# The order of every operation of an attention-and-mixer kernel written out as a list, in place of a list scheduler's choice

## The chip, the cores and the metric

The kernel runs on one core of a Trainium2 chip. The metric is device time in microseconds (us) of one execution, lower is better. A core has five engines that run at the same time: PE (TensorE, matrix products), ACT (ScalarE), DVE (VectorE), POOL (GpSimd) and SP (SyncE). Each takes its own instructions in the order in which the program issued them; semaphores tie the engines to each other. POOL and SP here issue almost only DMAs, ACT a few.

## The reference

Two networks, one behind the other, on q, k, v of 8 batches × 8 heads × 576 rows × 64:

```python
scores = scale * np.matmul(q, k.transpose(0, 1, 3, 2))
bias = slopes[:, None, None] * (-np.abs(rel).astype(np.float32))[None, :, :]
mask = (rel >= 0) & (rel < window)            # window = 128
scores = np.where(mask, scores + bias[None], -1000000000.0)
attn = softmax(scores);  out = np.matmul(attn, v)
x = out.transpose(0, 2, 1, 3).reshape(B, S, H * D)          # 8 x 576 x 512
xt = x.transpose(0, 2, 1)
h = np.maximum(xt @ w_tok1, 0.0) @ w_tok2                    # 576 -> 256 -> 576
u = x + h.transpose(0, 2, 1)
h2 = np.maximum(u @ w_ch1, 0.0) @ w_ch2                      # 512 -> 1536 -> 512
return u + h2
```

So a causal attention with a window of 128 and a bias that falls with the distance, then a mixer over the 576 tokens, then one over the 512 channels. Inputs and output are float32.

## The kernel before, in words

Products are in bf16 with float32 sums in PSUM. The 576 rows of a batch are four blocks of 128 and a tail of 64. Batches are worked on in pairs, and the two tails of a pair share one block (`TAIL`). `opening` does the attention and token mix of batch 0 by pairs of heads, so that work can start on the first loads. Then, for each batch `b`, `main(b)` is the channel mixer of that batch and `side(b + 1)` the attention and token mix of the next; their operations are interleaved. A block of `side` goes: loads by POOL; q and k turned, by a DMA transpose that SP issues (L761) or by products with the identity on PE (L772); scores (L809); exponential on ACT (L824) and mask on DVE (L834); value product (L897), whose 65th column is the sum; reciprocal (L910) and normalization, on DVE (L913, one operation) or ACT (L919, one for each head). The token mix has the products with W1 (L944) and W2, and `u` is written to `ub` (L1005) and turned by SP (L1013). `main` multiplies `uT` with WC1 in units (L1402, L1502), copies and adds what comes out on ACT or DVE (L1417, L1418, L1426 to L1430, L1508, L1509), and multiplies with WC2 (L1679).

In the opening the pairs of heads have their own lines: bias by a product (L1089), turns (L1063), scores (L1106), values (L1149), the score, value and normalization of the tail (L1194, L1220, L1227), and the token mix (L1243 with W1 and L1248 with its last 64 rows `W1p`, L1271 with W2). POOL's loads there are `load_pair` (L623, L630), `weights` (L635) and `load` (L614).

Nothing is issued directly. Each step is recorded as an operation (`plan.op`), 1486 in all, with its engine, a cost in ns, what it needs, the buffers it makes and uses, a rank, and sometimes a second engine that could do it (`other`). Buffers come from rings of a few slots: `ps` (8 PSUM banks), `qk`, `v`, `qkT`, `pe`, `rt`, `r`, `s`, `raw` and more; in the lists below `v_72` is a slot. A buffer's next owner has to wait for the last reader of the one before it.

`Plan.run` is a list scheduler. It steps through a modelled time; for each engine it takes the ready operation that can start earliest, ties going to the lower rank; it chooses the engine of operations with two, and the slot that is free first. POOL's operations keep one fixed order (`slot()`). A table, `NUDGES`, shifts the rank of single operations or holds them until a modelled time ("611:-21079:100923" is operation 611, rank, time); random shifts of the ranks are there too, with seeds that are all 0. `Plan.emit` then issues everything in order of the modelled start, and puts matmuls of a tile of zeros (`spin`, L1737) into those idle stretches of the modelled PE that begin before a set time, 60 us, and are longer than 250 ns, where a bank is free:

```python
        for a, z in self.gaps:
            if a < FILL and z - a > 250:
```

```python
    plan.run()
    plan.emit(spin)
```

Of the kernel before, what the change touches and what calls it, by code (L numbers as in the profile page):

```python
# [16 lines left out]
SEM = 40.0  # L17
# [54 lines left out]
class Plan:  # L72
# [60 lines left out]
    def run(self):  # L133
        ops = self.ops
        for item in NUDGES.split():
            n, rank, after = item.split(":")
            ops[int(n)].rank += float(rank)
            ops[int(n)].after = max(ops[int(n)].after, float(after))
        dice = [random.Random(x) for x in SEEDS]
        for o in ops:  # L140
            if SEEDS[o.part]:
                o.rank += dice[o.part].uniform(-SHIFT, SHIFT)
        succ = {o: [] for o in ops}
        left, held = {}, []
        ready = {o: o.after for o in ops}
        cand = {e: [] for e in ("PE", "ACT", "DVE", "POOL", "SP")}

        def enter(o):
            if any(x.t0 is None for x in o.behind):
                held.append(o)  # L150
                return
            cand[o.eng].append(o)
            if o.other:
                cand[o.other[0]].append(o)

        for o in ops:
            left[o] = len(o.deps)
            for d in o.deps:
                succ[d].append(o)
            if not o.deps:  # L160
                enter(o)
        pool = sorted((o for o in ops if o.eng == "POOL"), key=lambda o: o.order)
        free = dict(FREE)
        lanes, sent, turns = [], 0, []
# [5 lines left out]
        def finish(o):  # L170
            for h in list(held):
                if o in h.behind and all(x.t0 is not None for x in h.behind):
                    held.remove(h)
                    enter(h)

        def release(o):
            for s in succ[o]:
                left[s] -= 1
                ready[s] = max(ready[s], free["PE"] if o.eng == "PE" == s.eng else o.done + SEM)
                if not left[s]:  # L180
                    enter(s)

        def advance(to):
            nonlocal clock, flying
            while True:
# [11 lines left out]
                both = lines[0] and lines[1]  # L197
                rate = BOTH[lines[1][0][1].bus > 0] if both else (1.0, 1.0)
# [17 lines left out]
        def send(o, at, line, work, late):  # L216
            nonlocal flying
            coming.append([at, line, work, o, late])
            flying += 1

        while todo:
            best = None
            for e, c in cand.items():
                pick, early = None, None
                for o in c:
                    if e == "POOL" and o is not pool[sent]:
                        continue
                    t = max(ready[o], free[e])
                    if e == "DVE" and (o.narrow or last[0]):
                        t = max(t, last[1] + 31.0)  # L230
                    if o.other:
                        mine, its = (o.cost, o.other[1]) if e == o.eng else (o.other[1], o.cost)
                        that = o.other[0] if e == o.eng else o.eng
                        if max(ready[o], free[that]) + its < t + mine - (0 if e == o.eng else 1):
                            continue
                    asked = []
                    for b in o.bufs:
                        if b.slot is None:
                            opts = b.options()
                            got = b.ring.best(opts, asked.count(opts))  # L240
                            asked.append(opts)
                            if got is None:
                                t = None
                                break
                            t = max(t, got[0])
                    if t is None:
                        continue
                    if e == "POOL" and len(lanes) >= 8:
                        if lanes[-8].done is None:
                            continue  # L250
                        t = max(t, lanes[-8].done)
                    if e == "SP" and o.bus > 0 and len(turns) > 1 and turns[-2].done is None:
                        continue
                    own = o.rank - (ALIKE if e == "PE" and o.mode == mode != 0 else 0)
                    key = (t if t > free[e] + 1e-6 else free[e], own, o.n)
                    if pick is None or key < pick[0]:
                        pick = (key, o)
                    if o.rank < FIRST and (early is None or key < early[0]):
                        early = (key, o)
                if early and early[1] is not pick[1] and early[0][0] < pick[0][0] + GRACE * pick[1].cost:  # L260
                    pick = early
                if pick and (best is None or pick[0][0] < best[0][0]):
                    best = pick + (e,)
# [155 lines left out]
ALIKE = 0  # L419
# [1352 lines left out]
```

## Time and profile before

| what | value |
|---|---|
| times of the runs, us | 273.66, 274.33, 275.8; median 274.33 |
| span of the profiled execution, us | 272.2 (no time of this execution beside its span is given) |
| last matmul ends, us from the span's start | 268.53 |
| PE busy, matmuls recorded / weight loads | 263.6 us (97%), 2965 / 2992 |
| DVE, ACT, POOL busy | 224.7 (83%), 150.7 (55%), 114.7 (42%) |
| share of the chain that ended last | PE 90%, DMA 3%, POOL 3% |
| granted TensorE clock | 1.00 in every stretch looked at |

The span runs from the first to the last instruction of the core; the time is counted from outside and is longer. Every matmul comes with a weight load of its own, so the count of weight loads is that of matmuls; 27 matmuls have no record. A row of the lists of waits says which engine and line stood idle, what released it, and then us in total, times and the longest. In a timeline, a row's "x4" puts several instructions of a kind together.

### The profile page before, as it was taken

The numbers are of one execution on the slowest core, as the hardware profiler recorded it, in microseconds if no ns is written. First come the engines' busy times: TensorE is split into PE (matmuls) and PEld (weight loads), VectorE is DVE, ScalarE is ACT, GpSimd is POOL, SyncE is SP. The second block draws the span as 40 slices with busy tenths as digits, with TensorE's granted clock in tenths as the row PEclk, the third lists the DMA queues.
The fourth block names the chain that finished last, engine by engine and source line by source line (L and its number), as shares of the span: only waits on it lengthen the run. The fifth ranks groups of instructions, "written<-read, shape, count | busy, mean of one in ns | idle before, by whom it ended". The sixth has DMA issues, their size and how long they took to land.

```text
span 272.2 us, 7391 instructions
## 1 busy us (share of the span) xinstructions
PE 263.6 (97%) x2965; PEld 191.8 (70%) x2992; DVE 224.7 (83%) x520; ACT 150.7 (55%) x267; POOL 114.7 (42%) x147
## 2 busy tenths in 40 slices
PE   7989999999999999999999999999999999999994
PEld 5767566676686655587786756498886758589883
DVE  7887699978897569688999478698998989976983
ACT  6973796226881298107992089308973089506700
POOL 8978796840397007800870307800651050004000
PEclk9999999999999999999999999999999999999999
DMA  8999999999999979999999999999999580035005
GB/s 201 178 173 180 167 148 183 157 156 175 186 127 161 192 162 78 137 119 210 200 149 119 142 228 96 140 154 142 212 132 67 110 239 2 2 82 171 4 10 183
DMA packets 160338, 38.59 MB, mean 142 GB/s; under 512 B 146544, under 2 KB 159472, under 8 KB 160304
## 3 DMA queue, kind: packets, MB, share of 16 engines
q0 software_dynamic: 109968, 19.64, 89.4%
q1 hardware_dynamic: 49104, 17.70, 33.4%
q10 hardware_dynamic: 1232, 0.79, 1.0%
q8 instruction: 23, 0.38, 0.5%
q14 instruction: 11, 0.09, 0.1%
HBM read 35.85 MB, written 9.44 MB: 166 GB/s over the span
## 4 chain that ended last, share of the span: by engine, by line
PE 90%; DMA 3%; POOL 3%; issue 1%; ACT 1%; DVE 0%; POOLq 0%
PE ps L1679 27%; PE ps L1502 15%; PE ps L1402 12%; PE ps L897 6%; PE ps L809 5%; PE ps L987 4%; PE ps L944 4%; PE ps L1545 4%; PE ps L1590 4%; DMA W<-in_moe_w_tok_dram 2%; POOL v L623 1%; DMA qkT<-qk 1%; POOL qk L630 1%; PE ps L772 1%; PE ps L1488 1%
## 5 line engine op out<-in xcount | busy, mean ns | idle before, releaser
L614 POOL DMA_DIRECT2D v<-in_v_dram x36 | 30.5, 849 | 76.4 <-PE ps L897 72.8
L824 ACT ACTIVATE pe<-ps 128x1024 bf16<-128x1024 f32 (+1 forms) x56 | 51.3, 969 | 3.1 <-PE ps L809 3.0
L1502 PE MATMUL ps<-uT,WC 128*128 128x512 bf16 x182 | 46.0, 379 | 0.7 <-issue 0.2
L1508 ACT ACTIVATE r<-ps 128x512 bf16<-128x512 f32 x45 | 26.4, 601 | 35.9 <-PE ps L1502 33.8
L1679 PEld LDWEIGHTS <-r 128*128 128x128 bf16 x384 | 36.8, 98 | 7.4 <-issue 0.7
L1679 PEld LDWEIGHTS <-s 128*128 128x128 bf16 x288 | 27.8, 98 | 5.8 <-DVE s L1527 0.4
L614 POOL DMA_DIRECT2D qk<-in_k_dram x35 | 30.3, 873 | 3.7 <-DMA qk<-in_k_dram 1.6
L834 DVE TENSOR_TENSOR pe<-pe,mask 128x1024 bf16<-128x1024 bf16 (+1 forms) x48 | 30.5, 650 | 1.6 <-ACT pe L824 1.4
L614 POOL DMA_DIRECT2D qk<-in_q_dram x35 | 30.2, 867 | 3.7 <-DMA qkT<-qk 1.7
L1502 PEld LDWEIGHTS <-WC 128*128 128x128 bf16 x196 | 17.7, 98 | 18.1 <-issue 0.5
L1417 ACT COPY raw<-ps 128x512 f32<-128x512 f32 x27 | 15.5, 597 | 22.6 <-PE ps L1402 22.6
L1679 PE MATMUL ps<-WC,r 128*128 128x256 bf16 x192 | 24.9, 273 | 0.0
L1679 PE MATMUL ps<-WT,s 128*128 128x256 bf16 x192 | 24.7, 273 | 0.0
L1679 PE MATMUL ps<-WT,r 128*128 128x256 bf16 x192 | 23.8, 273 | 0.1
L897 PEld LDWEIGHTS <-pe 128*128 128x128 bf16 (+1 forms) x480 | 19.5, 99 | 5.6 <-DVE pe L834 0.8
L1426 DVE TENSOR_TENSOR r<-ps,raw 128x512 bf16<-128x512 f32 x30 | 20.2, 680 | 3.3 <-ACT raw L1417 2.8
L897 PE MATMUL ps<-v,pe 128*128 128x65 bf16 (+1 forms) x480 | 22.8, 194 | 0.1
L1005 DVE TENSOR_TENSOR ub<-ps,xb 128x512 bf16<-128x512 f32 x32 | 20.5, 683 | 2.7 <-ACT r L1508 0.9
L913 DVE TENSOR_TENSOR xb<-ps,rt 128x256 bf16<-128x256 f32 (+1 forms) x52 | 21.4, 417 | 0.5
L1650 DVE TENSOR_TENSOR raw<-ps,ub 128x512 f32<-128x512 f32 x25 | 17.0, 686 | 5.8 <-PE ps L1679 5.8
L1402 PE MATMUL ps<-tt,WS 128*128 128x256 bf16 x132 | 18.8, 273 | 0.1
L809 PEld LDWEIGHTS <-qkT 64*128 64x128 bf16 x448 | 11.9, 94 | 8.3 <-issue 5.9
(143 smaller groups left out, 479.4 us busy)
## 6 DMA issues: line engine op xcount, KB each, us to landing
out_dram<-raw SPq DMA_DIRECT2D x19, 256.0 KB, 4.4
qk<-in_q_dram POOLq DMA_DIRECT2D x30, 128.0 KB, 5.4
qk<-in_k_dram POOLq DMA_DIRECT2D x30, 128.0 KB, 5.4
v<-in_v_dram POOLq DMA_DIRECT2D x28, 128.0 KB, 5.1
WC<-in_moe_w_ch_dram POOLq DMA_DIRECT2D x8, 384.0 KB, 7.5
out_dram<-raw POOLq DMA_DIRECT2D x6, 256.0 KB, 3.4
out_dram<-ob SPq DMA_DIRECT2D x5, 256.0 KB, 4.1
v<-in_v_dram POOLq DMA_DIRECT2D x16, 64.0 KB, 4.8
```

The costliest lines, as they stand in the source:

```text
L614: nc.gpsimd.dma_start(out=to()[p0 : p0 + n, :, :], in_=rows(src, b, s0, n))
L809: pe_.matmul(wide(e)[:, i, kind, a:z], lhsT=ts[kb]()[e * D : (e + 1) * D, NHP + i, :], rhs=ts[blk]()[e * D : (e + 1) * D, i, a:z], start=T ...
L824: act_.activation(out=pb()[:, e, :, lo:, c0:c1_], in_=wide(e)[:, :, lo:, c0:c1_], func=ACT.Exp, scale=scale)
L834: dve_.tensor_tensor(out=o, in0=o, in1=heads(mk, es), op=ALU.mult)
L897: pe_.matmul(view()[a:z, at, i, :], lhsT=pb()[:, e, i, kind, a:z], rhs=vb()[:, h, 0 : D + 1], start=m == 0, stop=m == len(mms) - 1, skip_g ...
L913: dve_.tensor_tensor(out=x4(), in0=view()[r0:r1_, :, :, 0:D], in1=rt()[r0:r1_, 0:n, :, :].broadcast_to([r1_ - r0, n, 4, D]), op=ALU.mult)
L1005: plan.op("DVE", 690, lambda blk=blk, ht=ht, hs=hs: dve_.tensor_tensor(out=ub()[:, blk, :], in0=ht()[:, hs], in1=xb()[:, blk, :], op=ALU.a ...
L1402: pe_.matmul(bk()[:, c * HS : (c + 1) * HS], lhsT=l(c, cb), rhs=r(cb), start=new and c == 0 and cb == 0, stop=cb == 1, skip_group_check=True)
L1426: add = plan.op("DVE", 690, lambda: dve_.tensor_tensor(out=o(), in0=half_of(bk), in1=half_of(e), op=ALU.add), rk + UNIT_RANK, uses=[bk, e] ...
L1502: pe_.matmul(ct()[:, :], lhsT=WC1[:, cb, t * P : (t + 1) * P], rhs=uT()[:, cb, :], start=cb == 0, stop=cb == NCB - 1)
L1508: plan.op("ACT", 600, lambda t=t, ct=ct: act_.activation(out=r2()[:, t, :], in_=ct()[:, :], func=ACT.Relu), rk, part=(r2, t), uses=[ct], o ...
L1679: pe_.matmul(bk()[:, c * HN : (c + 1) * HN], lhsT=l(t, c), rhs=w(t), start=first, stop=g == 1 and t == HK - 1, skip_group_check=True)
```

## The change

The scheduler goes. `Plan.follow` takes three tables: `ORDER`, the numbers of all 1486 operations (in base 36) in the order in which they are placed; `ELSEWHERE`, the operations that run on their second engine; and `PLACES`, the first slot of each buffer in the order in which buffers first appear. Each engine's queue is what `ORDER` leaves for it. A replay of that order, with the same costs as before and two more waits in the model (280 ns after POOL's lane, 650 ns after a transpose on SP), gives each operation a modelled start, and `emit` still issues by these and still fills modelled gaps of PE. `NUDGES`, `SEEDS`, `SHIFT`, `FIRST`, `GRACE` and `ALIKE` are gone. No operation is added or removed; 59 run on the other engine, and the fills go from 52 matmuls to 49. The file is 20 lines shorter ahead of the code, so a line L1220 of before is L1200 now.

```diff
-    def run(self):
-        ops = self.ops
-        for item in NUDGES.split():
...
+    def follow(self):
+        def number(x):
+            return int(x, 36)
+
+        ops, seq = self.ops, [self.ops[number(x)] for x in ORDER.split()]
+        assert sorted(o.n for o in seq) == list(range(len(ops)))
+        for x in ELSEWHERE.split():
+            o = ops[number(x)]
+            o.eng, o.cost, o.emit = o.other
+        line = {e: [o for o in seq if o.eng == e] for e in ("PE", "ACT", "DVE", "POOL", "SP")}
...
+        places = iter(PLACES)
+        for o in seq:
+            for b in o.bufs:
+                if b.slot is None:
+                    first = number(next(places))
+                    b.slot = tuple(range(first, first + len(b.choice[0])))
+                    for i in b.slot:
+                        if b.ring.owner[i]:
+                            behind[o].append(b.ring.owner[i])
+                        b.ring.owner[i] = b
+                        b.ring.log[i].append(b)
+        ready, free = {o: o.after if o.after < 9e3 else 0.0 for o in ops}, dict(FREE)
...
+        def earliest(e, o):
+            if left[o] or any(u.done is None for b in behind[o] for u in b.users):
+                return None
+            t = max([ready[o], free[e]] + [u.done + SEM for b in behind[o] for u in b.users])
...
         while todo:
             best = None
...
+            for e, q in line.items():
+                if at[e] < len(q):
+                    t = earliest(e, q[at[e]])
+                    if t is not None and (best is None or t < best[0]):
+                        best = (t, e)
...
-NUDGES = ("611:-21079:100923 615:-377:0 618:6245:106227 624:11583:0 628:-3532:0 631:-20512:118175 632:4405:0 "
...
+ORDER = ("m i 52 4z d g 7 8 f 9 e a 4v 4x h k j n o l 1 2 6 4w 4y 3 50 51 5 57 53 55 58 56 c b 5c 59 5a 54 5b 5d 5i 5f "
...
+ELSEWHERE = ("4w 4y 5m 63 6f 6i 6x 7b 7m 84 86 88 8o 8q a5 at b6 bc bd c0 c2 c4 c8 ce cg cm cy fc fp fs fw gh gj gl gn gp "
...
-    plan.run()
+    plan.follow()
     plan.emit(spin)
```

The tables move instructions on every engine. Three places follow, each as it stands in before and then as it stands now.

POOL, the loads of the opening: `W_120` is W1, `W_122` W2, `W1p` the last 64 rows of W1, and the `v` buffers hold the values of batch 0's pairs of heads and its tail. Before:

```order
L623 DMA v_74<-in_v_dram 128x4x64 x2
L630 DMA qk_70<-in_q_dram 128x2x256
L630 DMA qk_70<-in_k_dram 128x2x256
L614 DMA v_73<-in_v_dram 64x8x64
L635 DMA W_120<-in_moe_w_tok_dram 128x4x256
L635 DMA W1p<-in_moe_w_tok_dram 64x256
L623 DMA v_75<-in_v_dram 128x4x64 x2
L623 DMA v_76<-in_v_dram 128x4x64 x2
L635 DMA W_122<-in_moe_w_tok_dram 128x2x512
```

Now:

```order
L610 DMA qk_68<-in_q_dram 128x2x256
L610 DMA qk_68<-in_k_dram 128x2x256
L603 DMA v_73<-in_v_dram 128x4x64
L615 DMA W_120<-in_moe_w_tok_dram 128x4x256
L603 DMA v_72<-in_v_dram 128x4x64 x2
L615 DMA W_122<-in_moe_w_tok_dram 128x2x512
L603 DMA v_75<-in_v_dram 128x4x64
L594 DMA v_76<-in_v_dram 64x8x64
L603 DMA v_75<-in_v_dram 128x4x64
L615 DMA W1p<-in_moe_w_tok_dram 64x256
```

W2 has moved ahead of the last three loads of values, the tail's values (64x8x64) have moved back from ahead of W1 to next to last of them, and W1's last rows have moved behind them all.

PE, at the end of the tail's value products (`pe_84` and `pe_86` hold the tail's exponentials, `pe_85` a block's). Before:

```order
L1220 MATMUL ps<-v_76,pe_84 64x65
L1220 LDWEIGHTS pe_84
L1220 MATMUL ps<-v_73,pe_84 64x65
L1737 LDWEIGHTS zero
L1737 MATMUL ps<-zero 128x512
L1737 LDWEIGHTS zero
L1737 MATMUL ps<-zero 128x512
L1737 LDWEIGHTS zero
L1737 MATMUL ps<-zero 128x128
```

Now:

```order
L1200 MATMUL ps<-v_75,pe_86 64x65
L1200 LDWEIGHTS pe_86
L1200 MATMUL ps<-v_76,pe_86 64x65
L1223 LDWEIGHTS W_120
L1223 MATMUL ps<-xb_91,W_120 128x128
L1223 LDWEIGHTS W_120
L1223 MATMUL ps<-xb_91,W_120 128x128
```

Two blocks of eight products with W1 stood ahead of the tail's value products; now all of them stand behind, the first of them where two wide and five narrow products with `zero` stood, and three narrow ones follow it. Further on, near 43 us of the span before, six narrow products with `zero` stood between the last value product of a tail (L897) and the token mix (L944); there are none after the opening now, and the token mix's first products stand among the value products of other blocks.

SP, around the transposes of one batch's `u` in the middle of the program (`uT`, `uTt`). Before:

```order
L1606 DMA out_dram<-raw_105 64x512 x2
L1013 DMA_TRANSPOSE uTt_100<-ub_93 128x4x128
L1013 DMA_TRANSPOSE uT_99<-ub_93 128x4x128 x4
L761 DMA_TRANSPOSE qkT_78<-qk_69 128x8x128
L761 DMA_TRANSPOSE qkT_83<-qk_71 128x8x128
L1662 DMA out_dram<-raw_107 128x2x256
L761 DMA_TRANSPOSE qkT_77<-qk_67 128x8x128
```

Now:

```order
L741 DMA_TRANSPOSE qkT_77<-qk_70 128x8x128
L741 DMA_TRANSPOSE qkT_78<-qk_71 128x8x128
L1642 DMA out_dram<-raw_105 128x2x256
L1642 DMA out_dram<-ob_109 128x2x256
L1642 DMA out_dram<-raw_106 128x2x256
L741 DMA_TRANSPOSE qkT_80<-qk_67 128x8x128
L1642 DMA out_dram<-raw_104 128x2x256
L1586 DMA out_dram<-raw_108 64x512
L1642 DMA out_dram<-raw_107 128x2x256
L741 DMA_TRANSPOSE qkT_79<-qk_69 128x8x128
L993 DMA_TRANSPOSE uT_98<-ub_93 128x4x128 x4
L993 DMA_TRANSPOSE uTt_100<-ub_93 128x4x128
```

The transpose that came first behind the `uT` group (`qkT_78` before) is the one just ahead of it now (`qkT_79`), and two more that followed the group now precede it (`qkT_80`, `qkT_77`).

More of the change, by code (lines that the diff above doesn't have):

```diff
@@ L131, in dma @@
         return o
-    def run(self):
-        ops = self.ops
-        for item in NUDGES.split():
[L136 to L139, printed above, removed]
-        for o in ops:
[L141 to L157, printed above, removed]
+    def follow(self):
[7 more added lines that the diff above has]
+        line = {e: [o for o in seq if o.eng == e] for e in ("PE", "ACT", "DVE", "POOL", "SP")}
+        succ = {o: [] for o in ops}
+        left = {o: len(o.deps) for o in ops}
+        behind = {o: [] for o in ops}
+        for o in ops:
@@ L168, in run @@
         lines, coming, clock, flying = ([], []), [], START, 0
[L170 to L174, printed above, removed]
         def release(o):
@@ L221, in run @@
         while todo:
             best = None
[L223 to L263, printed above, removed]
@@ L267, in run @@
             assert best, ("stuck", todo)
[L268 to L273 removed]
+            t, e = best
+            o = line[e][at[e]]
+            at[e] += 1
             todo -= 1
[L275 to L277 removed]
             if e == "PE":
```

98 lines of the change are left out of this document (34 added, 64 removed), and 42 rows, old and new, of the table ORDER.

## The prediction, made before the changed kernel was run

> **What bounds the kernel now.** The page first: busy shares over the whole span.
>
> ```profile
> span 272.2 us, 7391 instructions
> PE 263.6 (97%) x2965; PEld 191.8 (70%) x2992; DVE 224.7 (83%) x520; ACT 150.7 (55%) x267; POOL 114.7 (42%) x147
> ```
>
> TensorE (PE) is busy for 97% of the span. Its weight loads number 2992 and its matmuls 2965, so 27 matmul records are missing, and some of the 8.6 us (272.2 − 263.6) that look idle are not. The table by stage says where idle time can be at all (each row: stretch, its length, then busy time and count of PE, weight load, DVE, ACT, POOL, the granted clock, DMA share, GB/s).
>
> ```profile
> 0.00:20.00 20.00, 17.30 (x295) 12.95 (x295) 16.38 (x60) 15.15 (x29) 17.55 (x28) 1.00 1.44 184
> 30.00:100.00 70.00, 69.42 (x761) 46.08 (x771) 57.78 (x131) 40.98 (x71) 35.60 (x44) 1.00 1.75 169
> 100.00:150.00 50.00, 49.13 (x554) 35.99 (x558) 44.35 (x102) 29.09 (x50) 22.53 (x27) 1.00 1.38 138
> 150.00:240.00 90.00, 89.37 (x957) 64.09 (x966) 76.57 (x171) 51.11 (x93) 27.50 (x35) 1.00 1.02 128
> 240.00:268.53 28.53, 28.53 (x285) 25.58 (x283) 21.65 (x42) 10.12 (x18) 2.86 (x4) 1.00 0.27 84
> 268.53:272.20 3.67, 0.00 (x0) 0.00 (x0) 0.42 (x1) 0.00 (x0) 0.00 (x0) 1.00 0.40 119
> ```
>
> The first 20 us hold 2.70 us of idle PE. The three long stretches show 0.58, 0.87 and 0.63, together 2.08 us in 210, at the full granted clock. The last 28.5 us hold none, and the 3.67 us behind the last matmul are an add and a store that the change leaves in their order. PE's own waits name the causes (releaser; us in total, times, longest).
>
> ```profile
> PE ps L1737 <- DVE zero L565: 1.0, 1, 1.0
> PE ps L1243 <- DMA W<-in_moe_w_tok_dram: 0.6, 1, 0.6
> PE ps L1220 <- ACT pe L1114: 0.5, 1, 0.5
> PE ps L809 <- DMA qkT<-qk: 0.4, 1, 0.4
> ```
>
> The first is the start of the program and stays. The others are the largest idle times that a better order could remove (smaller ones follow in that view); beside them stand the matmuls on `zero`, which are time that PE spends on nothing.
>
> **The change part by part.** The same 532 groups of PE work are issued in both kernels. Matmuls go from 2992 to 2989, all of it fills (52 to 49), so the real work is 2940 in each. The change can move the time only through idle time, through fills and through the engines that PE waits for.
>
> *The opening.* The chain of waits (start, us, what):
>
> ```profile
> 8.19 5.95 DMA W<-in_moe_w_tok_dram
> ...
> 17.37 0.67 PE ps L1220 x16
> 18.03 0.82 PE ps L1737 x7
> 18.85 0.56 PE ps L1149 x14
> 19.40 0.34 PE ps L1737 x6
> 19.74 0.33 PE ps L1248 x4
> ```
>
> W1's load is issued at 8.19 and releases PE at 14.13; that 0.6 wait goes, since W1's first product now stands behind L1220. What ends last there instead are the v loads that L1220 reads. POOL issued them, and W2, so (start, us; then size and us to landing, from the issues near 12.5 us):
>
> ```profile
> 9.60 3.02 POOL L623 DMA_DIRECT2D v<-in_v_dram  x4
> 12.56 0.75 POOL L635 DMA_DIRECT2D W<-in_moe_w_tok_dram  x1
> W<-in_moe_w_tok_dram POOLq DMA_DIRECT2D x1, 256.0 KB, 5.6
> v<-in_v_dram POOLq DMA_DIRECT2D x1, 64.0 KB, 4.2
> ```
>
> The last v load is issued at about 9.60 + 3.02 × 3/4 = 11.9 and lands at 11.9 + 4.2 = 16.1; W2, next in line, lands at 12.56 + 5.6 = 18.2. So 256 KB cost the line 18.2 − 16.1 = 2.1 us. In the new order W2 stands ahead of the last three loads that L1220 reads and W1's 32 KB tail goes behind them. The last of them lands near 16.1 + 2.1 − 0.2 = 18.0 (32 KB at that rate are 0.26), where PE had L1220 done at 17.37 + 0.67 = 18.04. Since only L1220's last products read it, L1220 ends about 0.1 later. Behind L1220 the fills (0.82 + 0.34 = 1.16) are partly replaced by two blocks of W1 products that stood ahead of it, but the product that follows, L1248 at 19.74, waits for DVE's norm of L1220's result, 1.7 us after its end, in either order. The cover for the moved blocks is therefore this gap, and what they free lies ahead of L1220, where the v load now decides. I take −0.2 for the opening. The ends: −1.1 if the v loads come in time (0.6 of wait and 0.5 of wait both gone), +0.7 if the last v load comes a whole 64 KB (2.1 / 4 = 0.5) behind W2, at 18.2 + 0.5 = 18.7.
>
> Four wide bias matmuls also move out of the first five microseconds. Their prices (start, us; then the same line later):
>
> ```profile
> 2.59 2.32 PE L1089 MATMUL ps<-dist,slant 128*128 128x128 bf16 x12 [0.24 <-DVE slant L582]
> 8.19 0.60 PE L1089 MATMUL ps<-dist,slant 128*128 128x256 bf16 x4
> ```
>
> The early twelve are 8 of 256 columns and 4 of 128, 2560 columns or 0.91 ns each; the later four take 0.60 / 1024 = 0.59 ns a column. Early there are now 6 wide and 2 narrow, 768 columns fewer, worth 768 × 0.32 = 0.25 us, but fills take their place there and the qk loads set when the next work starts, so I count 0, between −0.25 and 0. [...]
>
> *The fill at 43 us.*
>
> ```profile
> 43.05 0.69 PE L897 MATMUL ps<-v,pe 128*64 128x65 bf16 x16
> 43.68 0.51 PE L1737 MATMUL ps<-zero 128*128 128x128 bf16 x6
> 44.04 1.24 PE L944 MATMUL ps<-xb,W 128*128 128x512 bf16 x4
> ```
>
> From 43.68 to 44.04 PE multiplies zeros while DVE normalizes the tail that L944 waits for. Now L944's first products are spread among the value products and no fill stands there: −0.4, or 0 if the wait remains and merely shows as idle.
>
> *The transposes near 121 us.*
>
> ```profile
> 115.07 6.03 SPq L1013 DMA_TRANSPOSE uT<-ub  x4
> 121.27 2.61 SPq L761 DMA_TRANSPOSE qkT<-qk  x2
> 124.52 0.23 PE L809 MATMUL ps<-qkT 64*128 64x128 bf16 x2 [0.42 <-DMA qkT<-qk]
> ```
>
> SP issues in its own order, so qkT waited behind the 6.03 us of uT, and L809 stood 0.42 for it. In the new order this qkT and two more go out ahead of the uT group: −0.4. What is late next is uT itself, pushed by one issue, 2.61 / 2 = 1.3 us, if SP reaches the new place only when `ub` is ready; its first reader would then wait up to 1.3. SP's rows show it waiting for `ub`, not being late for it, so the issue fits into that wait:
>
> ```profile
> SPq L1013 <- DVE ub L1005: 56.2, 8, 18.7
> ```
>
> *Operations on their other engine (59).* Prices, mean ns of one:
>
> ```profile
> L1418 DVE COPY raw<-ps 128x512 f32<-128x512 f32 x3 | 2.1, 686 | 0.0
> L913 DVE TENSOR_TENSOR xb<-ps,rt 128x256 bf16<-128x256 f32 x50 | 20.6, 417 | 0.5
> L1417 ACT COPY raw<-ps 128x512 f32<-128x512 f32 x27 | 15.5, 597 | 22.6 <-PE ps L1402 22.6
> L919 ACT ACTIVATE xb<-ps,rt 128x64 bf16<-128x64 f32 x48 | 11.1, 333 | 0.5 <-DVE rt L910 0.4
> ```
>
> DVE takes 14 more full-bank copies and relus at about 0.686 = 9.6, and loses 12 half-bank operations at 0.417 (8 norms and 4 copies of uT) = 5.0 and two relus at 0.686 = 1.4: about +3.2 us. ACT takes 32 pieces of norms at 0.333 = 10.7 and seven copies and relus at about 0.6 = 4.2, and loses 16 at 0.6 = 9.6: about +5.3. ACT's 55% hide that; a moved norm takes 4 × 0.333 = 1.3 on ACT where DVE took 0.417, which is covered only while PE has other work. DVE is the tighter:
>
> ```profile
> 116.00:146.00 30.00, 29.33 (x371) 23.96 (x372) 27.39 (x63) 19.82 (x36) 11.04 (x13) 1.00 1.46 167
> ```
>
> Here 2.6 us of 30 are free on DVE. The 3.2 us are spread over some 200 us, so they fit on average; for new short waits I add +0.2, between 0 and +1.6 (half of the 3.2).
>
> The sum: −0.2 − 0.4 − 0.4 + 0.2 = −0.8 us. No time of the profiled execution but its span is given; the median of the runs, 274.33, lies 2.1 above it, and the same is taken to lie around the new one. So 274.33 − 0.8 = 273.5, a span of about 271.4.
>
> **The rivals.**
>
> *A larger gain.* The v loads come in time and every small idle goes: −1.1 in the opening, −0.25, −0.4, −0.4, and half of the 2.08 us less the 0.42 already counted, −0.8; together −2.9, 271.4, and 270.5 to 272.5 around it. For it: no wait of PE after 20 us but L809's is over 0.4. Against it: the missing 27 records at about 0.11 us are 3.0 us, more than all idle after 20 us, so there may be little to gain. A row shows how dense the work is (chain; 48 matmuls of 256 columns):
>
> ```profile
> 239.65 5.24 PE ps L1679 x48
> ```
>
> That is 109 ns each, back to back. [...]
>
> *DVE becomes the bound.* If half of its added work falls where DVE has no room, +1.6 more on the path than none: 273.5 + 1.4 = 274.9, and 274.5 to 276.0. It decides from 2.6 us more in such a 30 us stretch. For it: 91% there. Against it: norms leave DVE in the same stages.
>
> *Slower: POOL's queue holds.* POOL issues loads in order, and a v load waits until PE has read the old v:
>
> ```profile
> POOL v L614 <- PE ps L897: 72.8, 12, 15.7
> qk<-in_k_dram POOLq DMA_DIRECT2D x30, 128.0 KB, 5.4
> ```
>
> A k load behind it needs 5.4 us to land and some 3 us as a transpose before PE can use it, about 8.5. The new order mixes loads of several blocks. If one such k load is released 8.5 − 4 = 4.5 us or less before its use instead of in time, PE stands some 4 us: 273.5 + 4 = 277.5 (276 to 278). It decides once a release comes later than 8.5 us before the product. Against it: with the old queue the only such wait was 0.42, and qkT mostly goes out earlier now.
>
> *No effect.* Every gain is taken back by the next thing in line, since loads and norms and not the list set the moments: 274.3.
>
> **How the numbers follow.** About 1% (2.7 us) is what a measurement tells from no change here; the three runs alone differ by 2.1. The forecast has 0.45 (272.5 to 274.5), the larger gain 0.22, DVE 0.18, POOL 0.09, no effect 0.06. Faster by over 1% is below 271.6: some 0.6 of the larger gain, 0.13. Slower by over 1% is above 277.1: most of POOL's and a little of DVE's, 0.10. Within 1%: 0.77. The range leaves out the lower half of the larger gain (0.1) and POOL's (0.09): 271.4 to 276.0.
>
> **What would show it.** Right: no L809 wait for qkT near 121 us; no `zero` matmul after 21 us; L1200 (the new number of L1220) ending within 0.3 us of 18.0 and waiting for a v load; PE busy 97% again. Wrong: in the opening, L1200 ending after 18.7 or before 17; in the middle, PE waits named DVE of over 0.5 us together (DVE's rival); a new wait for qkT of over 1 us (POOL's). If the last matmul ends before 265.6 or after 271.3, the sum has missed a term.

## The result, and the profile after

| | before | after |
|---|---|---|
| median of the runs, us | 274.37 (6 runs, 273.66 to 275.8) | 278.47 (6 runs, 277.13 to 280.29) |
| ratio, 95% interval | | 1.0155 (1.0123 to 1.0188) |
| span of the profiled execution, us | 272.2 | 275.9 (the time of that run is 277.71, 1.8 above) |
| mean granted clock, all runs | 1.000 in the profiled one | 0.985 to 0.994 |

The kernel became slower by 4.1 us; 273.5 had been forecast. The first lines of the page of the kernel after:

```profile
span 275.9 us, 7370 instructions
PE 264.5 (96%) x2962; PEld 192.5 (70%) x2989; DVE 228.1 (83%) x521; ACT 151.8 (55%) x290; POOL 114.6 (42%) x147
```

PE's busy time rose by 0.9 us and the span by 3.7, so most of the loss is idle PE. DVE has 3.4 us more, ACT 1.1. The stretches (columns as in the prediction) show where the idle time is:

```profile
0.00:20.00 20.00, 17.31 (x277) 12.75 (x278) 14.91 (x51) 14.60 (x28) 16.11 (x26) 0.91 1.44 183
8.00:12.00 4.00, 4.00 (x57) 2.80 (x54) 2.40 (x4) 2.22 (x4) 3.81 (x6) 0.59 1.58 188
20.00:30.00 10.00, 9.85 (x139) 7.60 (x140) 7.48 (x21) 5.42 (x14) 10.00 (x13) 1.00 1.96 165
30.00:100.00 70.00, 66.49 (x730) 44.57 (x740) 56.28 (x124) 42.05 (x77) 39.26 (x50) 1.00 1.61 147
100.00:150.00 50.00, 49.53 (x559) 35.58 (x564) 44.94 (x104) 29.18 (x55) 20.50 (x25) 1.00 1.53 165
150.00:240.00 90.00, 89.27 (x959) 64.64 (x967) 76.08 (x169) 53.06 (x104) 25.87 (x33) 1.00 1.01 130
```

From 30 to 100 us PE stands 3.51 us where it stood 0.58; from 100 on the stretches are as dense as before. And there is a second, smaller sign at the beginning: PE is just as busy in the first 20 us, but at a mean clock of 0.91; from 8 to 12 us it was granted 0.59. PE's waits name the large idle time:

```profile
PE ps L1482 <- DMA WC<-in_moe_w_ch_dram: 2.1, 1, 2.1
PE ps L1043 <- DVE qk L627: 1.1, 2, 0.9
PE ps L789 <- DVE qkT L758: 0.6, 1, 0.6
```

The first is a wait for a load of the channel mixer's weights, WC1; no such wait was in the profile before. It stands at 30.20 to 32.29 us, and the third right behind it (timeline of PE, start and duration, in brackets the idle time ahead):

```profile
29.82 0.38 PE L1468 MATMUL ps<-uT,WC 128*128 128x512 bf16 x1
32.29 1.04 PE L1482 MATMUL ps<-uT,WC 128*128 128x512 bf16 x4 [2.09 <-DMA WC<-in_moe_w_ch_dram]
33.88 0.23 PE L789 MATMUL ps<-qkT 64*128 64x128 bf16 x2 [0.55 <-DVE qkT L758]
```

L1482 is the line that was L1502: one chunk of `main(0)`, four products with 128 columns of WC1. Before, it began at once, at 29.28:

```profile
29.28 1.02 PE L1502 MATMUL ps<-uT,WC 128*128 128x512 bf16 x4
```

POOL's timeline shows why the load is late (L615 issues weights, L594 a load of q, k or v):

```profile
13.67 0.81 POOL L615 DMA_DIRECT2D WC<-in_moe_w_ch_dram  x1
16.17 0.82 POOL L615 DMA_DIRECT2D WC<-in_moe_w_ch_dram  x1
19.30 0.89 POOL L594 DMA_DIRECT2D v<-in_v_dram  x1 [2.30 <-PE ps L1200]
...
25.41 0.80 POOL L615 DMA_DIRECT2D WC<-in_moe_w_ch_dram  x1
```

WC1 comes in four loads of 384 columns (384 KB each). The third of them is issued at 25.41, behind seven loads of v, q and k, of which the first stood 2.30 us for PE to read the old v. From the issues near 25.4:

```profile
WC<-in_moe_w_ch_dram POOLq DMA_DIRECT2D x1, 384.0 KB, 6.8
```

25.41 + 6.8 = 32.2, where L1482 starts. In the kernel before the first three of these loads went out at 13.24, 16.44 and 18.98:

```profile
13.24 0.83 POOL L635 DMA_DIRECT2D WC<-in_moe_w_ch_dram  x1
16.44 0.78 POOL L635 DMA_DIRECT2D WC<-in_moe_w_ch_dram  x1
18.98 0.77 POOL L635 DMA_DIRECT2D WC<-in_moe_w_ch_dram  x1
```

DVE waits for the same load, for its sums of weights (L707), and holds a copy behind that has nothing to do with it: the `qkT` (L758) for which PE stands the further 0.55.

```profile
DVE WS L707 <- DMA WC<-in_moe_w_ch_dram: 2.8, 1, 2.8
```

Added up at the first L1482: PE arrives at 30.20 instead of 29.28 (+0.92, the opening), waits 2.09 and then 0.55, together 3.56 of the 3.7 us of span. The clock did not fall behind this wait; in this execution it fell in the opening only.

Why did the order put a load so late that is needed so early? The code has the answer. A chunk `t` reads `WC1[:, cb, t * P : (t + 1) * P]` and records `needs=[lc1[t]]`. But `lc1` is filled in the order of the table `LOADS`, which names the four loads as `A0 … A2 … A1 … A3`. So `lc1[6]` is load `A1`, columns 384 to 767, while chunk 6, the first of this line, reads columns 768 to 895, load `A2`. The recorded need is the wrong load. Before, `A2` was the second to be issued and `A1` the third, so a chunk that waited for `A1` had `A2` as well. The new `ORDER` has `A1` second and `A2` third (numbers `12` and `10`), and nothing in the replay, which knows only the record, says that this is early. On the chip PE's wait went by what the instruction reads: in b_wc, below, `A1` is issued at 24.15 and the chunk starts at 29.26 all the same, without a wait. In the program as built, the third load writes the columns from 768 on and raises a semaphore, and the first weight load of L1482 reads those columns and waits for that semaphore (shortened):

```
POOL  L615 DMA WC_124         [its queue's lane: semaphore DMASW3]     third WC load of the new order
PE    L1482 LDWEIGHTS WC_124  [waits DMASW3_49]
```

### The profile page after: what moved, and what is told of

It is laid out like the page before. It is cut to its first block, busy times and chain, and to the rows that moved or that the text cites. A ratio compares the mean times of both kernels' runs of the same rounds, so it can differ in the third digit from the quotient of the medians.

```text
span 275.9 us, 7370 instructions
## 1 busy us (share of the span) xinstructions
PE 264.5 (96%) x2962; PEld 192.5 (70%) x2989; DVE 228.1 (83%) x521; ACT 151.8 (55%) x290; POOL 114.6 (42%) x147
## 5 line engine op out<-in xcount | busy, mean ns | idle before, releaser
L804 ACT ACTIVATE pe<-ps 128x1024 bf16<-128x1024 f32 (+1 forms) x56 | 52.0, 977 | 9.7 <-PE ps L789 9.6
L1482 PE MATMUL ps<-uT,WC 128*128 128x512 bf16 x183 | 46.2, 380 | 2.8 <-DMA WC<-in_moe_w_ch_dram 2.1
L594 POOL DMA_DIRECT2D v<-in_v_dram x36 | 31.2, 870 | 40.0 <-PE ps L877 37.2
L594 POOL DMA_DIRECT2D qk<-in_q_dram x35 | 30.4, 880 | 30.5 <-DMA qkT<-qk 30.5
L594 POOL DMA_DIRECT2D qk<-in_k_dram x35 | 30.4, 875 | 27.3 <-DMA qkT<-qk 27.3
L1488 ACT ACTIVATE r<-ps 128x512 bf16<-128x512 f32 x39 | 22.7, 603 | 32.2 <-PE ps L1482 31.8
L1482 PEld LDWEIGHTS <-WC 128*128 128x128 bf16 x196 | 17.4, 98 | 20.1 <-DMA WC<-in_moe_w_ch_dram 2.4
L877 PEld LDWEIGHTS <-pe 128*128 128x128 bf16 (+1 forms) x480 | 20.8, 99 | 6.7 <-DVE pe L814 0.6
L1659 PE MATMUL ps<-WC,r 128*128 128x256 bf16 x192 | 25.4, 273 | 0.0
L877 PE MATMUL ps<-v,pe 128*128 128x65 bf16 (+1 forms) x480 | 24.0, 194 | 0.2
L899 ACT ACTIVATE xb<-ps,rt 128x64 bf16<-128x64 f32 (+1 forms) x76 | 17.6, 321 | 11.8 <-DVE rt L890 11.8
L1630 DVE TENSOR_TENSOR raw<-ps,ub 128x512 f32<-128x512 f32 x26 | 17.8, 685 | 5.2 <-PE ps L1659 5.0
L1397 ACT COPY raw<-ps 128x512 f32<-128x512 f32 x20 | 11.6, 598 | 16.1 <-PE ps L1382 10.8
L1642 POOL DMA_DIRECT2D out_dram<-raw x6 | 4.3, 721 | 36.7 <-issue 25.4
L1406 DVE TENSOR_TENSOR r<-ps,raw 128x512 bf16<-128x512 f32 x27 | 18.2, 683 | 1.4 <-PE ps L1382 0.8
```

The lines of the kernel that those rows point to most:

```text
L594: nc.gpsimd.dma_start(out=to()[p0 : p0 + n, :, :], in_=rows(src, b, s0, n))
L804: act_.activation(out=pb()[:, e, :, lo:, c0:c1_], in_=wide(e)[:, :, lo:, c0:c1_], func=ACT.Exp, scale=scale)
L877: pe_.matmul(view()[a:z, at, i, :], lhsT=pb()[:, e, i, kind, a:z], rhs=vb()[:, h, 0 : D + 1], start=m == 0, stop=m == len(mms) - 1, skip_g ...
L899: act_.activation(out=x4()[:, e, i, :], in_=view()[r0:r1_, e, i, 0:D], func=ACT.Copy, scale=rt()[r0:r1_, e, i, :])
L1406: add = plan.op("DVE", 690, lambda: dve_.tensor_tensor(out=o(), in0=half_of(bk), in1=half_of(e), op=ALU.add), rk + UNIT_RANK, uses=[bk, e] ...
L1482: pe_.matmul(ct()[:, :], lhsT=WC1[:, cb, t * P : (t + 1) * P], rhs=uT()[:, cb, :], start=cb == 0, stop=cb == NCB - 1)
```

## The experiments

The theory to be tested was that POOL's queue, with the late WC load, makes the whole loss. Its rivals: that the opening and its clock make it (the bias products moved out of the first microseconds); that the 59 moved operations, DVE's added work above all, make it; and that the new code itself costs something. Each time is given with its ratio to runs of before taken together with it, and the interval of that ratio. Where an expectation has a letter for a theory, Q stands for the queue and D for DVE and the engines.

All kernels named `a…` start from the changed kernel, with its fills kept in place; those named `b…` are the order, engines and slots of before, written into the new tables. Their files are 4 to 6 lines longer: L1488, L1487 and L1486 are L1482, and L758, L795, L883 and L1206 are L752, L789, L877 and L1200.

### The wanted load moved ahead (a_wc)

```diff
-ORDER: 12 11 13 1c 14 17 18 15 10
+ORDER: 12 10 11 13 1c 14 17 18 15
```

> One edit to the changed kernel: in POOL's queue the third quarter of WC1 (a load of 384 KB) goes ahead of the seven loads of v, q and k that stand before it, to directly behind the second quarter. PE's order and the fills are those of the changed kernel. Theory Q (POOL's queue): the first of the seven, a v load, waits until PE has read the old v (2.30 us in the trace), so this quarter is issued at 25.41 and PE waits 2.1 us for it (L1482), and 0.55 more for a copy that stands on DVE behind the sums that wait for it. Without this: 278.5 - 2.6 = 275.9, no wait of PE for WC over 0.5. Theory C (the clock in the opening is all, the WC wait would only be moved elsewhere): 278 to 278.5. Rival D (more work on DVE): 278.5, no change.

Measured: 274.08 us (10 runs), 0.9985 of before (0.9965 to 1.0005). The wait for WC is gone, and with it 4.4 us, more than the 2.6 of the two waits and than the 275.9 that was expected. In most executions a lower clock goes with it: all runs of the change have a mean clock of 0.985 to 0.994, nine of the ten runs here 0.997 to 1.000. What is left of the change is level with before. PE's row for the same chunk:

```profile
30.27 1.03 PE L1488 MATMUL ps<-uT,WC 128*128 128x512 bf16 x4
```

It still starts 1 us later than before: this profile has the slow opening of the kernel after (clock 0.57 from 8 to 12 us). By 272.6 us, its span, all but 0.4 of that is made good.

### Only the two loads exchanged (a_swap)

```diff
-ORDER: 12 11 13 1c 14 17 18 15 10
+ORDER: 10 11 13 1c 14 17 18 15 12
```

> The changed kernel with two loads exchanged in POOL's queue, nothing else: the second and the third load of WC1 (the one of columns 384 to 767, issued at 16.17, and the one of columns 768 to 1151, issued at 25.41). Theory N (which load): the first product of the seventh chunk, L1482, multiplies columns 768 and up, so what PE waits for is that load alone, and the other is wanted only from 32 us on: with the two exchanged the wait of 2.1 is gone, 0.3 at most comes for the other: 274.0 to 275.0. Theory Q (a late load of WC1, whichever it is): 278 to 278.5.

Measured: **272.83 us (12 runs, 272.13 to 274.84), 0.9959 of before (0.9939 to 0.9978)**. This is faster than both kernels, by 0.4% of before and by 2% of the change. Everything else of the change is in it. Its page, its waits after 20 us (one), and the chunk:

```profile
span 270.5 us, 7398 instructions
PE 264.8 (98%) x2989; PEld 192.1 (71%) x2989; DVE 228.3 (84%) x521; ACT 152.0 (56%) x290; POOL 114.6 (42%) x147
```

```profile
PE ps L758 <- DMA qk<-in_k_dram: 0.2, 1, 0.2
```

```profile
28.38 1.03 PE L1488 MATMUL ps<-uT,WC 128*128 128x512 bf16 x4
```

So with a good opening the new order reaches the first chunk 0.9 us earlier than before, and it keeps that. That an exchange of two issues, which leaves their number and POOL's work as a whole as they were, is worth 5.0 us (against 277.86 for the change once more, measured together with it, below) to 5.6 (against 278.47) settles the main question. The gain is larger than the theory had it (274.0 to 275.0). `A1`, now the late one, is issued at 24.51 and lands 7.5 us later, at 32.0; the first product that reads it starts at 32.09 without a wait, so the exchange fits with nothing to spare:

```profile
32.09 1.04 PE L1488 MATMUL ps<-uT,WC 128*128 128x512 bf16 x4
```

From 36 to 100 and from 150 to 240 us PE has no idle time left:

```profile
36.00:100.00 64.00, 64.00 (x704) 42.64 (x702) 52.22 (x114) 39.26 (x79) 35.91 (x44) 1.00 1.71 157
150.00:240.00 90.00, 90.00 (x973) 64.64 (x971) 77.47 (x171) 53.09 (x104) 25.88 (x33) 1.00 0.98 129
```

### The order of before in the new code (b_list)

```diff
-ORDER, ELSEWHERE, PLACES of the change
+the order, engines and slots that the list scheduler of before came to
```

> The order, engines and buffers of before, written into the tables of the changed kernel and issued by its code (four fills more, all else in before's order). All theories on the order: as before, 274.0 to 274.9. If anything but the order (the replay, the way of issuing) costs time: above 275.5.

Measured: 274.40 us (10 runs), 1.0000 of before (0.9977 to 1.0024). The machinery of the tables costs nothing. One detail: this kernel's profile has no wait for `qkT` at the score product at 124.52 us, the 0.42 of the prediction. But the next two kernels, b_wc and b_wc36, which have PE's order of before too, have it again, 0.62 and 0.46 at the same product:

```profile
PE ps L794 <- DMA qkT<-qk: 0.6, 1, 0.6
PE ps L794 <- DMA qkT<-qk: 0.5, 1, 0.5
```

So it stands in three of four executions with this order.

### The wrong load made late (b_wc)

```diff
-ORDER of before: the third WC load (12) and the fourth (16) in their places
+both behind the next block's loads; the fills that the replay adds from 20 to 42 us left out
```

> Before's order (274.4) with one part of the change alone: in POOL's queue the third quarter of WC1 goes behind the seven loads of v, q and k that follow it, and the fourth quarter with it, as they stand in the changed kernel. Theory Q: the quarter is issued near 25.1 in place of 19.06, lands 7 us later at 32, and PE, which wants it at 29.4, waits 2.6 us, with 0.5 more behind it on DVE: 277 to 278.5. Theory that the wait comes from the new order as a whole (a later opening): no wait over 0.5, 274.4 to 275.

Measured: 273.92 us (10 runs), 0.9997 (0.9975 to 1.002). A miss, and the most useful one. The third load by position is issued at 24.15 instead of 18.98, and PE does not care:

```profile
24.15 1.56 POOL L620 DMA_DIRECT2D WC<-in_moe_w_ch_dram  x2
```

```profile
29.26 1.02 PE L1487 MATMUL ps<-uT,WC 128*128 128x512 bf16 x4
```

In the order of before the third load is `A1`, in the new one it is `A2`. I had taken "the third load" for the wanted one, as the recorded need says. Only this result led to the columns that a chunk reads.

### The right load made late (b_wc36)

```diff
-ORDER of before: A2 (10) as the second WC load
+A2 behind nine loads; the same fills left out
```

> Before's order (274.4), in POOL's queue the second load of WC1 (columns 768 to 1151) alone goes behind the nine loads of q, k and v that follow it; the third and fourth load of WC1 stay. Theory N: it is issued near 28 in place of 16.5 and lands near 34; PE wants it at 29.3, waits 4 to 5 us, and the clock falls to 0.50 behind so long a wait: 279 to 282. If only the new order is hurt by a late load: 274.4.

Measured: 283.11 us (4 runs), 1.0313 (1.0285 to 1.0341), above the range I gave. POOL, PE, and two of the stretches:

```profile
26.99 0.86 POOL L620 DMA_DIRECT2D WC<-in_moe_w_ch_dram  x1
```

```profile
35.28 1.89 PE L1487 MATMUL ps<-uT,WC 128*128 128x512 bf16 x4 [6.41 <-DMA WC<-in_moe_w_ch_dram]
```

```profile
36.00:38.00 2.00, 2.00 (x19) 0.92 (x17) 0.00 (x0) 0.60 (x1) 1.63 (x3) 0.50 1.52 197
```

With everything else as before, this one load makes PE wait 6.41 us; and behind the wait the four products take 1.89 us instead of 1.02, at a granted clock of 0.50. The expectation had the fall of the clock; what it had too small was the wait, 4 to 5 us: the load, issued at 26.99, took 8.2 us to land, where about 6 had been put.

### The change once more (after_again)

```diff
 (no edit: the changed kernel)
```

> The changed kernel once more, instruction for instruction, for a second profile: the wait of L1482 for WC again 1.5 to 3.5 us, 277 to 280.5; where the wait is over 3 us the granted clock is 0.50 behind it, where it is about 2 it is not.

Measured: 277.86 us (4 runs), 1.0128 (1.0095 to 1.016). The profile is of a good opening, and shows how the loss is made then:

```profile
30.89 1.88 PE L1488 MATMUL ps<-uT,WC 128*128 128x512 bf16 x4 [2.65 <-DMA WC<-in_moe_w_ch_dram]
```

```profile
32.00:34.00 2.00, 2.00 (x19) 0.91 (x18) 2.00 (x5) 0.22 (x1) 1.83 (x3) 0.50 1.88 181
```

PE arrives at 30.89 − 2.65 = 28.24, 1.0 us ahead of before, and waits longer, since the load comes when it comes. Then the clock falls: 0.73, 0.50 and 0.91 in the three stretches of 2 us from 30 to 36, which is (0.27 + 0.50 + 0.09) × 2 = 1.7 us of full speed at most. So −1.0 + 2.65 + 1.7 + 0.61 (a wait for `qkT` near 91 us) = +4.0; the span is 276.2, 4.0 above before. The sum is rough: a wait of 0.4 for `xb`, and what the new order gains behind the chunk (0.8 us in a_swap: 1.7 by the spans less 0.9 at the chunk), are not in it. The expectation had put the fall of the clock behind waits of over 3 us; here it came behind 2.65, and in a_bias, below, behind 2.06. And since a_swap, with as good an opening, is 5.0 us faster, the opening does not make the loss.

### More work for PE in the opening (a_fills)

```diff
-fills of 4 and 7 zero products in the opening
+fills of 12 and 11
```

> One edit to the changed kernel: 8 more products with zero ahead of the first turn (12 in place of 4) and 4 more ahead of the first score (11 in place of 7); nothing that is computed moves. Theory C: the same clock as with the bias products moved back, 1.00 from 8 to 11 us; 276.5 to 277.8 though PE does 12 matmuls more. If the clock stays down or the products only delay the turns: 278.5 to 279.3. Rival D: 278.5.

Measured: 280.87 us (4 runs), 1.0219 (1.0169 to 1.0268). The clock is 1.00 from 4 to 12 us here, PE reaches the chunk at 28.12, and so it waits 3.21:

```profile
31.33 1.28 PE L1488 MATMUL ps<-uT,WC 128*128 128x512 bf16 x4 [3.21 <-DMA WC<-in_moe_w_ch_dram]
```

```profile
32.00:34.00 2.00, 1.65 (x18) 0.89 (x18) 2.00 (x6) 0.00 (x1) 1.44 (x3) 0.50 2.13 169
```

The time is above every range that was given. The clock falls behind that wait, and once more near 110 us, behind a wait of 1.91 for `qkT` (0.62 and 0.52 from 110 to 114); why that wait comes here and not in the change itself no run shows. An earlier opening gives nothing while the load sets the moment. What the fills alone are worth it does not show: after_again, without them, has a clock of 1.00 from 4 to 12 us as well, and reaches the chunk at 28.24.

### Both together, and DVE's first work reordered (aw_fills, aw_best, aw_dve)

```diff
 aw_fills: a_wc with the fills of a_fills
 aw_best:  aw_fills, and ORDER: DVE's clearing of qk and the slopes' identity (f, e) ahead of its first cast (7)
 aw_dve:   a_wc with that order of DVE, fills as they were
```

> The changed kernel with the load of WC1's third quarter moved forward (274.1 by itself) and the 12 more products with zero in the opening, that brought the clock to 1.00 from 8 to 12 us there but no time. Theory Q: with the load early, PE no longer waits for it, so what the opening gains at 28 us (1.1 us behind before's order) now stays: 273.0 to 273.5. If the loads of the opening set its end whatever the clock: 273.9 to 274.3, as without the products.

> As the run before (aw_fills), and on DVE two small operations (a memset of 0.48 us and a scaled identity of 0.21) go ahead of the four casts of q and k, into the time in which DVE waits for the first of them, as in before's order. If DVE's casts set the opening's start: 0.3 to 0.6 less than aw_fills, 272.6 to 273.2. If the transfers of q and k set it: equal to aw_fills within 0.3.

> The changed kernel with the load of columns 768 to 1151 moved forward (274.1), and on DVE the memset and the scaled identity ahead of the four casts of q and k, without more products with zero. If a faster opening only makes PE run into later loads: 274.1 to 276. If the opening's start is worth its time: 273.2 to 273.9.

Measured, 12 runs each: 276.70 (1.0096, 1.0066 to 1.0126), 276.55 (1.0071, 1.0047 to 1.0095) and 274.41 (1.0001, 0.9975 to 1.0026). None beats a_wc. aw_fills lies 2.4 us above the higher of its two ranges, aw_best is equal to it, as one theory had it, and aw_dve is at the low end of "only makes PE run into later loads". With the WC wait gone, aw_fills has new waits, for loads that stand behind the moved one:

```profile
28.32 0.28 PE L883 MATMUL ps<-v,pe 128*128 128x65 bf16 x4 [0.96 <-DMA v<-in_v_dram]
30.79 0.40 PE L758 MATMUL ps<-ident,qk 128*128 128x128 bf16 x4 [0.88 <-DMA qk<-in_k_dram]
```

The first of these waits ends when the first of the seven loads lands. POOL issues it behind two weight loads, and the issues near 18.5 us tell how long it took to land:

```profile
18.60 0.94 POOL L600 DMA_DIRECT2D v<-in_v_dram  x1
```

```profile
v<-in_v_dram POOLq DMA_DIRECT2D x1, 128.0 KB, 9.6
```

18.60 + 9.6 = 28.2. In a_swap only one weight load stands ahead of it:

```profile
17.36 0.89 POOL L600 DMA_DIRECT2D v<-in_v_dram  x1
```

```profile
v<-in_v_dram POOLq DMA_DIRECT2D x1, 128.0 KB, 7.7
```

17.36 + 7.7 = 25.1, which is 3.1 us earlier: 1.2 by the issue, 1.9 by a shorter time from issue to landing. That the 384 KB more ahead of it make those 1.9 is not shown: aw_dve and aw_best have the same two weight loads ahead of it, and there it lands 7.9 and 7.8 us after its issue. What the three have in common is the second line, the wait for the k load: 0.88, 0.72 and 0.61 in aw_fills, aw_dve and aw_best, 0.20 in a_swap. So moving `A2` ahead is not free where PE comes early; exchanging it with `A1`, which PE needs later, costs less. The profile of a_wc has no such wait: its opening was late, and PE came to these products later. Why the fills cost a_wc as much as 2.6 us in the median, and why the runs of aw_fills spread from 275.0 to 279.3, stays open: its profile has further waits of 0.6 and 0.7 in the middle of the program that no run took apart.

### The operations back on their old engines (aw_eng)

```diff
-ELSEWHERE of the change
+ELSEWHERE as the list scheduler of before chose (59 operations), order as in a_wc
```

> The changed kernel with the load of WC1's third quarter moved forward, and all 59 operations back on before's engines, each at its place in the new order; the order itself, the buffers and the fills stay. Theory Q: the engines are not what costs time; within 0.5 of 274.1, either way. Rival D (DVE's 3.3 us more are on the path and hidden in the 274.1 by gains elsewhere): 272.5 to 273.3.

Measured: 288.40 us (6 runs), 1.0519 (1.049 to 1.0548); no theory had said so. The new waits are spread:

```profile
PE ps L1664 <- DVE raw L1635: 3.1, 5, 1.7
PE ps L1387 <- ACT raw L1402: 1.5, 1, 1.5
```

This order, fixed for its own choice of engines, is a bad one for the other choice. So this run does not price the 59 moves; it shows only that order and engines were chosen as one.

### The bias products moved back (a_bias)

```diff
-ORDER: the first transposes of q and k (4v) ahead of the wide bias products (59)
+the group of bias products ahead of them, as before
```

> One edit to the changed kernel: on PE one group of bias products (6 matmuls, 1280 columns) goes back ahead of the first turn, where before had it (and the bank of that turn's result is another). Theory C: PE is then busy until the casts of q and k are there, the granted clock stays at 1.00 between 8 and 11 us, where it was 0.50 in the changed kernel; the opening ends about 0.9 earlier, and the WC load, held behind it, lands up to 1 us earlier: 276.5 to 277.6. Theory Q alone: the clock is incidental, the WC wait stays 2.1: 278.0 to 278.5. Rival D: 278.5.

Measured: 279.64 us (4 runs), 1.0195 (1.0144 to 1.0246). With the move, what the bias products add to the scores of the opening is not what it is in the other kernels, so the time is to be read with care. It was meant to show what the low clock of the opening is worth; instead PE stood 2.0 us for the scaled identity that those products read, so that question was not answered. The WC wait of 2.1 is there as in the changed kernel, and the clock fell to 0.52 behind it (34 to 36 us).

## Why the prediction was wrong, point by point

**The failing step** is the first of "the change part by part": the opening. It followed POOL's list as far as the ten rows that are shown with the change, priced W2 ahead of the v loads, and stopped there. The rows behind, in which the second and third WC loads changed places and the third went behind seven loads, were not read, so the sum lacks a term: 2.09 of wait, 0.55 of the copy that DVE held behind it, and in other executions a lower clock behind a longer wait (2.65 in after_again; every run had a mean clock of 0.994 or less). What a load pays for those put ahead of it was reckoned for the v loads and not for WC.

**Without that term the sum is near, in part by luck.** The forecast −0.8 gave 273.5; a_swap, the change with the wanted load early, gives 272.83, 1.3 below the runs of before taken together with it. By parts:

- *Opening, −0.2 (−1.1 to +0.7).* The size depends on when the first raw q and k loads land. With those on time, the first chunk is reached at 28.1 to 28.4 instead of 29.28, −0.9 to −1.2, in three profiles (a_swap, after_again, a_fills). In the two with the loads late it is reached at 30.2 and 30.3, +0.9 and +1.0. The reason given for −0.2 was wrong: the v loads did not come late behind W2. In a_swap the last of them is issued at 12.64 and lands some 4.5 us later, near 17.1, where 18.0 had been worked out, and L1206 starts at 16.59 and ends at 17.3; I had it end near 18.1. Of the bias products, four leave the first five microseconds, as was said, but two of them are wide and two narrow; the 768 columns are right.
- *The fill near 43 us, −0.4.* Between 40 and 45 us a_swap gains 0.33 on b_list at the same work, and no fill stands there. About right.
- *The `qkT` wait near 121 us, −0.4.* It is gone in the profile after, as forecast, and it was the old order's in three of four executions. What the sum did not have is that the new order has a wait for `qkT` near 90 us, in some executions only: 0.24 in the profile after, 0.61 in after_again, 0.68 in aw_fills, 1.09 in aw_dve, none in a_swap and a_wc.
- *New short waits, +0.2, and DVE as a rival.* DVE's work grew by 3.4, against 3.2. In a_swap it cost nothing: at the same work, that kernel is 1.59 us ahead of b_list at 45 us and 1.76 at 265, and no PE wait of over 0.2 us after 20 us names DVE there. The rival falls. (Single waits for DVE of 0.4 us stand in after_again and aw_fills.) ACT grew by 1.1, where +5.3 had been summed.
- *No effect.* Not so either: a_swap is 1.3 us faster than before.

**The POOL rival was right in kind.** It had POOL issue in order, a v load wait for PE, and a load behind it come late, at 277.5 (276 to 278), with a chance of 0.09; 278.47 came. But it looked for a k load, with "the only such wait was 0.42" as the evidence against it. That 278.47 lies close to its time is in part luck: the load was another, and in most executions part of the time is the clock. The load that came late is one that in the profile before is never waited for. From its issues near 16.4 us:

```profile
WC<-in_moe_w_ch_dram POOLq DMA_DIRECT2D x1, 384.0 KB, 7.4
```

It landed at 16.44 + 7.4 = 23.8, 5.4 us ahead of its use at 29.28. A profile of before shows no wait for what is early; how early it is has to be read from landing and first use.

**Range and chances.** The range ended at 276.0 by leaving out just this rival. The clock, which the prediction had at 1.00 throughout, took up to 1.7 us where it fell behind the wait in after_again, so a rival priced by the wait alone was also too cheap.

**What would show it.** Of the signs named, the L809 wait was gone as said, no `zero` product stands after 21 us, and a wait of L1200 for a v load was not there. L1200 ended at 19.2 in the profile after, past the 18.7 named as a sign of being wrong, and at 17.3 in a_swap, so what moved it was the late raw loads of q and k, not W2. The bound on the end decided: the sum has missed a term if the last matmul ends after 271.3, and it ended at 272.2.

## What to carry to other kernels

When an order is rewritten, list for each load of the moved queue its issue, its landing and its first reader in the old trace, and check each against its new place, those first that are never waited for. A scheduler sees only the needs that are recorded, and a need that names the wrong piece of a buffer can stay harmless until the order changes, as here; so compare what an operation reads with what it declares. Price a wait on PE with what the clock may do behind it (here up to 1.7 us in after_again), and look at more than one execution before a wait is called gone or new: the two waits for `qkT` come and go with the same order.

## What was not expected of the hardware

**The granted clock fell to 0.50 behind some of PE's waits, for 3.4 us, once for 6.8.** After the opening it fell behind waits of 1.91, 2.06, 2.65 and 3.21 us (a_fills, a_bias, after_again, a_fills) and within that of 6.41 (b_wc36), and not behind the 2.09 of the first profile after, nor behind any wait under 1.9. How long it stayed low is worked out from the rows of 2 us around each fall. In after_again 0.73, 0.50 and 0.91 are 1.7 us of full speed, which at 0.50 makes a low stretch of 3.4 us, from 30.9 to 34.4. a_bias (0.52 and 0.62 from 34 to 38) and the two of a_fills (0.50 and 0.65 from 32 to 36, 0.62 and 0.52 from 110 to 114) come to 3.4 too. b_wc36 (0.56, 0.50, 0.50 and 0.73 from 32 to 40) comes to 6.8, with PE still waiting in the first half, until 35.28. In the opening of the profile after, read in steps of 0.2 us, the low stretch goes from 7.85 to 11.26.

What decides whether it falls no run shows. The length of the wait alone does not: 2.06 was followed by a fall and 2.09 was not. The time that PE is busy does not either: from 30.2 to 33.6 us of the profile after PE was busy for 1.04 of 3.4 us and the clock stayed at 1.00, and from 4.4 to 7.85 us it was busy for 1.99 of 3.45 and the clock fell at the end. And in a_bias it was busy for 2.23 us from 4 to 8 us and the clock stayed at 1.00 to 12 us, where it fell behind 2.54 (after) and 2.39 (a_wc).

**The first loads of a run landed at different times.** The raw q and k loads of the opening are issued at the same place in all these kernels, and in twelve of fourteen profiles DVE's first two casts of them begin at 4.1 to 4.5 us and the third by 6.0. In the first profile after they begin at 4.85, after a wait of 1.40 for the load; in a_wc the third cast waits 1.11 and begins at 6.82. In these two PE stood longest for a cast in the opening (1.1 us together at L1043 in the profile after, 1.2 at L1049 in a_wc; the next is aw_eng with 0.6), and in these two the clock fell there (0.59 and 0.57 from 8 to 12 us).

**A load that one engine waited for delayed work of another.** In the profile after, DVE's 2.8 us for WC held back a copy of `qkT` that was ready, and PE stood 0.55 for that copy after its own wait for the same load was over.
